# Two-layer transformer kernel: the v projection of the last two layer-1 chunks by seven block products instead of eight, and an emission clock that counts free PSUM banks

## The chip, the core and the metric

The kernel runs on one NeuronCore of a Trainium2 chip. The metric is the device time of one launch in microseconds (us), the median of three runs. PE is TensorE (matrix multiplications; PEld is its weight load), DVE is VectorE, ACT is ScalarE, POOL is GpSimd, SP is SyncE, which here only issues DMAs.

## The reference, cut to what matters

`x` is 2048 tokens by 1024. Each of two layers adds an attention part A and a gated part B, both with the same weights in both layers:

```python
def _A_ref(x, wqkv, wo):          # 32 heads of 32; 8 keys, 2 apart, behind each token
    q, k, v = (x @ wqkv) split in three      # wqkv: 1024 x 3072
    ...                                      # softmax over 8 gathered keys, sum of 8 gathered values
    return o @ wo
def _B_ref(x, w1, w3, w2):        # w1, w3: 1024 x 3584; w2: 3584 x 1024
    return (silu(x @ w1) * (x @ w3)) @ w2
x = x + _A_ref(_layernorm(x), ...)
x = x + _B_ref(_layernorm(x), ...)
x = x + _A_ref(_layernorm(x), ...)
x = x + _B_ref(_layernorm(x), ...)
```

What the change touches is `x @ wqkv`, its last third (v), in layer 1.

## The kernel before

**Units.** The tokens are cut into four chunks of 512; a unit `u` is a layer and a chunk, so u = 0 to 3 is layer 0 and u = 4 to 7 is layer 1. After the four q, k, v products of layer 0, the main loop runs part B of each unit (`b_stage`), and after part B of u = 1, 2, 3, 4 it makes q, k, v of unit u + 3, a chunk of layer 1 (`q_part`, once for each of q, k, v). Every `q_part` takes eight output tiles of 128 rows, each from eight matmuls of 512 columns (L836), evacuated from PSUM by one ACT copy (L840), and written to DRAM; the attention reads q, k and v back from DRAM. One chunk's q, k, v is called a qkv stage here, and its three thirds the q, k and v third.

**Seven products.** From unit 2 on, part B doesn't multiply in the plain way. A product of 2 by 2 blocks is made from seven block products instead of eight (a scheme of the Strassen family): P1, P5, P6, P2 with weights from a tile `early`, P7, P3, P4 with weights from a tile `late`. The sums of weight blocks were made once, earlier (`weight_sums`, `differences`: ACT scales blocks into `big`, DVE adds them, POOL's DMAs store them in DRAM as `t_d`). The sums of the activations are four DVE additions over `xnT` (`norm_sums`, L298), the last of which, for P7, overwrites half of `xnT`. `pipeline` (L1034) runs groups of seven products (each eight matmuls of 256 columns, L1052), the first four products of group i interleaved with the last three of group i - 1. Between products stand small steps: ACT copies P1's result to a second bank (L1064, "B copy"), saves P5 (L1069) and P6 (L1073); DVE adds P6 to the bank of P5 (L1076) and makes one of the four outputs, the "corner", from P7 and P5 (L1088 or L1090). P6 and P2 wait for the B copy, P3 for L1076, P4 for the corner.

**Order.** PE, DVE, ACT and SP each execute their instructions in the order of the program. That order is decided while the kernel is built, by a clock `now` with a cost for each piece of work. Steps of attention, of the norms and of the sums stand in queues as generators; `background(until)` emits the DVE steps that end before the next DVE step of the main line is due, and `act_background` does so for ACT. So a wrong cost only shifts where a step stands, and an engine that reaches a step too early waits, with all that is queued behind it. The norm of a later unit on ACT is `act_norm`: two measuring passes per 128 tokens (L318), seven tiny POOL operations, then an applying pass (L345) and a DMA transpose into `xnT`.

**Attention.** DVE makes scores (L590, L510 and smaller) and values (L665 and smaller) of half chunks, in order; ACT makes one Exp per half chunk (L629), which needs another ACT table than the Silu of part B (L1227), so a table load stands before and after it. PE multiplies the outcome by `wo` (`o_tile`, L771).

**Buffers.** Weight tiles rotate over six buffers (`wp`), released by `release` and loaded by SP in the order of the list `seq`. PSUM has six banks for matrix products (tag `mm`) and two at the side (tag `sd`, for `wo` products and attention logits). The clock knows nothing of banks before the change. `hT` is part B's hidden tile, and the staging for q, k, v of layer 1.

Of the kernel before, what the change touches and what calls it, by code (L numbers as in the profile page):

```python
# [17 lines left out]
def kernel(  # L18
# [137 lines left out]
    opened = [0]  # L156

    def side_tile(*args, **kw):

        while opened[0]:  # L160
            assert head(makes) is not None
            take(makes)
        return side.tile(*args, **kw)

    def bank(name):
        if name == "po":
            return side_tile([P, 512], FP32, name=name, tag="sd")
        return psum.tile([P, 512], FP32, name=name, tag="mm")
# [48 lines left out]
    size2 = const.tile([P, 16], FP32, name="size2")  # L217
    total = const.tile([P, 1], FP32, name="total")
# [4 lines left out]
    h16 = hT[:].bitcast(FP16)  # L223
    t2_d = [dram.tile([P, 7, (b - a) // 2, 512], FP16, name=f"t2_d{i}") for i, (a, b) in enumerate(fsplits)]
    t_d = [[dram.tile([P, 14, KT // 2, P], FP16, name=f"t_d{m}_{g}") for g in range(NG)] for m in range(2)]
    qkv_d = [[dram.tile([P, KT, S], BF16, name=f"qkv_d{l}_{i}") for i in range(3)] for l in range(2)]
# [74 lines left out]
    adds, acts, makes, reads, parts, sizes = [], [], [], [], [], []  # L301
# [61 lines left out]
    def act_background():  # L363
        for queue in (acts, sizes, parts, reads):
# [211 lines left out]
    def score_steps():  # L576

        V = nc.vector
        for g, (l, h) in enumerate(halves):
# [20 lines left out]
            def gather_heads(t, parts_=parts_):  # L600
                at["L"] = L = side_tile([P, W, BLK], FP32, name="L", tag="sd")
                for i in range(parts_):
# [24 lines left out]
            def exps():  # L627
                V.tensor_tensor(L[:], L[:], mx[:].unsqueeze(1).to_broadcast([P, W, BLK]), op=ALU.subtract)
                nc.scalar.activation(E[:], L[:], ACTF.Exp, scale=scale)  # L629
                at["E"] = act(0.65, now["dve"] + 0.1, "exp")  # L630

# [47 lines left out]
    for u in range(len(units)):  # L679
# [14 lines left out]
        if 1 <= u and u + 3 < len(units):  # L694
            seq += [("qkv", which, h) for which in range(3) for h in range(2)]
    w_tiles, w_at, due, used = [], {}, [], [0]

    def load_weight(pieces=1):
# [25 lines left out]
        else:  # L724
# [4 lines left out]
            if rest[0]:  # L729
                got = {}  # L730
                parts.append([weight_size(*rest[0], w, at, got), None])
                reads.append([weight_sums(*rest[0], w, got), None])
# [22 lines left out]
    def o_tile():  # L755
# [12 lines left out]
        for hh in range(2):  # L768
            ps = bank("po")
            for t in range(KT):  # L770
# [6 lines left out]
            dve(0.64, r)  # L777
# [6 lines left out]
    def queue_q(q):  # L784
# [4 lines left out]
        
# [30 lines left out]
    def q_part(l, c, which, ws, then=()):  # L820
# [8 lines left out]
        for t0 in range(0, KT, SG):  # L829
            i = (c * 3 + which) * KT // SG + t0 // SG  # L830
            i = i % (7 if l == 0 else 8) * SG
            sgt = big[:, i * CH:(i + SG) * CH].bitcast(BF16).rearrange("p (a t) -> p a t", a=SG) if l == 0 else hT[:, i:i + SG, :]
            for t in range(t0, t0 + SG):
                ps = bank("ps")
                for kk in range(KT):
# [6 lines left out]
                if first:  # L842
                    nc.scalar.copy(kT[:, t, HALO:], ps[:, 0:TCH])
                    done = act(0.3)
                if t < t0 + SG - 1:
                    pe_requests(2)
            nc.sync.dma_start(qkv_d[l][which][:, t0:t0 + SG, c * CH:(c + 1) * CH], sgt)
            landed = dma(256, done)
            if l == 0:
                stored[:] = landed, landed  # L850
# [6 lines left out]
        if which == 1:  # L857
            plain_left.discard(("Q", l, c))
        if which == 2:
# [56 lines left out]
    pending, stored, made, held = [0] * 2, [0.0] * 2, set(), []  # L916
    junk = hsum[:].bitcast(BF16).rearrange("p k t -> p (k t)")

    def differences(m, g, a, r):

        b = blocks[a]
# [3 lines left out]
        pending[a] -= 1  # L925
        nc.gpsimd.dma_start(t_d[m][g][:, 4 * a:4 * (a + 1)], b[:, 0:4])
        nc.gpsimd.dma_start(t_d[m][g][:, 8 + 3 * a:8 + 3 * (a + 1)], b[:, 4:7])
        stored[a] = now["dve"] + 7.0

    def finish_sums(done):  # L930

        while not done():
            if head(reads) is not None:
                take_act(reads)
            elif head(parts) is not None:
                take_act(parts)
            elif head(makes) is not None:
                take(makes)
# [62 lines left out]
    def sums_of_w2(i, f, ws, loaded):  # L1001

        while "at" not in got2 or all(pending):
# [31 lines left out]
    def pipeline(key, groups, consume, done, last, fill=None):  # L1035
# [6 lines left out]
        def acc():  # L1042
            return psum.tile([P, 2, HT], FP32, name="st", tag="mm")
# [12 lines left out]
        def head_part(i, name):  # L1056
            G = groups[i]
            s5, su, s22 = snaps[i % 2], snaps[2], snaps[3]
            if name == "P1":
                G["early"] = weight("early")  # L1060
                G["A"] = acc()
                r = run(G, name, G["A"], True)
                G["B"] = acc()
                nc.scalar.copy(G["B"][:], G["A"][:])  # L1064
                G["tB"] = act(0.5, r)
            elif name == "P5":
                G["D"] = acc()
                r = run(G, name, G["D"], True)
# [9 lines left out]
            elif name == "P2":  # L1078
                r = run(G, name, G["B"], False, G["tB"])
                release(1)  # L1080
                consume(G, 0, G["B"][:], r)
# [11 lines left out]
            elif name == "P3":  # L1093
                r = run(G, name, G["D"], False, G["tD"])
                consume(G, 1, G["D"][:], r)
            else:
                r = run(G, name, G["A"], False, G["tC"])
                release(1)
                consume(G, 2, G["A"][:], r)

        n = len(groups)
        for i in range(n + 1):
# [15 lines left out]
            done(i)  # L1118

    def products(u, f0, f1, hold):  # L1120
# [25 lines left out]
        def output(j, hh, src, r):  # L1146
# [4 lines left out]
            dve(0.69, r)  # L1151
            if l == 1 and lastsplit:
                nc.sync.dma_start(xout[:, n, hh * 512:(hh + 1) * 512], xs)
                dma(128, now["dve"])

        def W(name, j):
# [12 lines left out]
            if name == "P1":  # L1169
                G["A"] = bank("w2")  # L1170
                r = G["1"] = matmuls(G["A"], True)
                G["B"] = bank("w2")
# [240 lines left out]
```

## Time and profile before

| what | value |
|---|---|
| median of three runs (lowest, highest) | 1533.35 us (1532.43, 1533.71) |
| the profiled execution's own time | 1532.7 us |
| its span, first to last instruction | 1531.0 us |
| busy in the span: PE, PEld | 1518.1 us (99%), 989.5 us |
| busy in the span: DVE, ACT, POOL | 1201.8 us (78%), 884.1 us (58%), 153.7 us |
| granted TensorE clock | 1.000 |
| DMA | 439.56 MB, 287 GB/s on average |

Busy time is the union of an engine's instructions; an instruction of PE is listed with its whole latency, so its mean is longer than the distance from one matmul to the next. "Idle before" is the time for which the engine stood still just before such an instruction, and the releaser is what ended that. The median of the runs is 2.4 us above the span.

### The profile page before, as it was taken

What the parts mean: (1) busy time and instruction counts of PE and PEld (TensorE: products, weight loads), DVE (VectorE), ACT (ScalarE), POOL (GpSimd) and SP (SyncE); (2) the same over time, 40 slices, a digit from 0 to 9 for tenths busy, and PEclk for the clock granted to TensorE, in tenths of its full rate; (3) what the DMA queues carried; (4) which work ended last, traced back from release to release, by engine and by line L of the source; (5) the groups of instructions that cost most, each with busy time, mean ns of one, the idle gap of its engine ahead of it and who ended that gap; (6) DMA issues with size and microseconds to landing.
All of it is one profiled execution on the core that took longest, in us unless ns stands there. A gap on an engine that the chain in (4) does not pass through costs nothing.

```text
span 1531.0 us, 25095 instructions
## 1 busy us (share of the span) xinstructions
PE 1518.1 (99%) x9594; PEld 989.5 (65%) x9634; DVE 1201.8 (78%) x2126; ACT 884.1 (58%) x1388; POOL 153.7 (10%) x308
## 2 busy tenths in 40 slices
PE   9999999999999999999999999999999999999999
PEld 7666644444444577575786767766677767686865
DVE  4688998889989898989698958898678986435445
ACT  3885476567665357455565564756557445554643
POOL 1210102121211101001011010100111000000000
PEclk9999999999999999999999999999999999999999
DMA  9777969798997888979779997898969988878885
GB/s 321 202 218 215 253 226 330 272 304 289 306 320 247 280 316 294 347 264 303 263 269 324 346 268 282 280 323 302 323 225 333 338 296 282 306 272 334 318 294 203
DMA packets 261432, 439.56 MB, mean 287 GB/s; under 512 B 73856, under 2 KB 201088, under 8 KB 245056
## 3 DMA queue, kind: packets, MB, share of 16 engines
q1 hardware_dynamic: 248464, 390.90, 76.8%
q0 software_dynamic: 12704, 46.93, 8.6%
q8 instruction: 75, 1.23, 0.3%
q14 instruction: 45, 0.37, 0.1%
q10 hardware_dynamic: 144, 0.13, 0.0%
HBM read 345.90 MB, written 67.90 MB: 270 GB/s over the span
## 4 chain that ended last, share of the span: by engine, by line
PE 97%; ACT 1%; issue 1%; DVE 0%; DMA 0%; SPq 0%; ACTq 0%
PE st L1052 32%; PE ps L836 21%; PE w L1165 16%; PE po L771 7%; PE pg L1279 6%; PE pu L1288 6%; PE acc L1310 6%; PE pq L444 1%; PE L L604 0%; DMA wqkv<-in_A_wqkv_dram 0%; ACT L629 0%; ACT L1227 0%; ACT E L629 0%; ACT sg L1227 0%; DVE x_sb L1150 0%
## 5 line engine op out<-in xcount | busy, mean ns | idle before, releaser
L836 PE MATMUL ps<-xnT,wqkv 128*128 128x512 f16 (+1 forms) x1469 | 320.4, 379 | 0.2
L1052 PEld LDWEIGHTS <-early 128*128 128x128 f16 x2688 | 262.6, 98 | 40.4 <-issue 3.5
L836 PEld LDWEIGHTS <-wqkv 128*128 128x128 bf16 x1472 | 210.6, 144 | 108.1 <-issue 2.2
L1165 PE MATMUL w<-t,hT 128*128 128x512 f16 x1008 | 226.0, 379 | 0.6 <-ACT big L1185 0.5
L1052 PEld LDWEIGHTS <-late 128*128 128x128 f16 x2016 | 197.2, 98 | 30.6 <-issue 2.5
L590 DVE TENSOR_TENSOR tree<-qT,kT 128x2048 bf16<-128x2048 bf16 x128 | 156.3, 1221 | 35.8 <-DMA kT<-qkv_d 18.2
L1052 PE MATMUL st<-xnT,late 128*128 128x256 f16 x1344 | 174.2, 273 | 2.2 <-ACT big L1073 2.2
L510 DVE TENSOR_TENSOR tree<-tree 128x1024 bf16<-128x1024 bf16 x256 | 175.6, 686 | 0.9
L1052 PE MATMUL st<-big,early 128*128 128x256 f16 x1344 | 172.3, 273 | 1.6 <-ACT sg L1227 1.1
L1165 PEld LDWEIGHTS <-hT 128*128 128x128 f16 x1008 | 98.2, 98 | 112.9 <-DVE hT L1136 2.0
L1052 PE MATMUL st<-xnT,early 128*128 128x256 f16 x1344 | 165.7, 273 | 0.0
L665 DVE TENSOR_TENSOR tree<-At,vT 128x2048 bf16<-128x2048 bf16 x128 | 156.2, 1221 | 11.9 <-DMA At<-E 10.7
L1064 ACT COPY st<-st 128x512 f32<-128x512 f32 x84 | 48.3, 575 | 128.1 <-PE st L1052 127.4
L771 PE MATMUL po<-wo,oT 128*128 128x512 bf16 x486 | 110.8, 379 | 1.3
L840 ACT CAST hT<-ps 128x512 bf16<-128x512 f32 x96 | 55.8, 585 | 90.6 <-PE ps L836 88.3
L1288 PE MATMUL pu<-xnT,w3t 128*128 128x512 f16 x448 | 105.8, 379 | 0.0
L1279 PE MATMUL pg<-xnT,w1t 128*128 128x512 f16 x448 | 105.8, 379 | 0.0
L1310 PE MATMUL acc<-w2t,hT 128*128 128x512 bf16 x437 | 97.8, 379 | 0.6
L1076 DVE TENSOR_TENSOR st<-st,big 128x512 f32<-128x512 f32 x84 | 58.4, 695 | 46.9 <-ACT big L1073 46.8
L1227 ACT ACTIVATE sg<-st,down_scale 128x512 bf16<-128x512 f32 x126 | 86.6, 687 | 11.6 <-PE st L1052 11.0
L1052 PE MATMUL st<-big,late 128*128 128x256 f16 x672 | 87.1, 273 | 0.0
L771 PEld LDWEIGHTS <-oT 128*128 128x128 bf16 x512 | 50.1, 98 | 55.7
(167 smaller groups left out, 1916.6 us busy)
## 6 DMA issues: line engine op xcount, KB each, us to landing
early<-t_d SPq DMA_DIRECT2D x84, 1024.0 KB, 6.9
late<-t_d SPq DMA_DIRECT2D x84, 768.0 KB, 6.2
t<-t_d SPq DMA_DIRECT2D x42, 1024.0 KB, 7.3
t<-t_d SPq DMA_DIRECT2D x42, 768.0 KB, 5.3
wqkv<-in_A_wqkv_dram SPq DMA_DIRECT2D x28, 1024.0 KB, 8.1
w1t<-in_B_w_dram SPq DMA_DIRECT2D x14, 1024.0 KB, 7.6
w3t<-in_B_w_dram SPq DMA_DIRECT2D x14, 1024.0 KB, 11.0
t_d<-big POOLq DMA_DIRECT2D x28, 512.0 KB, 6.2
```

Of the source, the lines that this page charges most:

```text
L510: nc.vector.tensor_tensor(b, b, buf[:, 4:8, :], op=ALU.add)
L590: V.tensor_tensor(pr, qT[:], kT[:, :, k0:k0 + TCH], op=ALU.mult)
L665: V.tensor_tensor(tm.rearrange("p w (a e) -> p w a e", a=4), At[:].rearrange("p a w e -> p w a e"), win, op=ALU.mult)
L771: nc.tensor.matmul(ps[:], lhsT=oT[:, t, j * P:(j + 1) * P], rhs=wo[:, t, hh * 512:(hh + 1) * 512], start=(t == 0), stop=(t == KT - 1))
L836: nc.tensor.matmul(ps[:], lhsT=ws[kk // KH][:, kk % KH, t::KT], rhs=xnT[:, kk, :], start=(kk == 0), stop=(kk == KT - 1))
L1052: nc.tensor.matmul(out[:, a, :], lhsT=w[:, a, blk, k, :], rhs=rhs[:, k, :], start=start and a == 0 and k == 0, stop=k == KQ - 1, skip_grou ...
L1076: nc.vector.tensor_tensor(G["D"][:], G["D"][:], su, op=ALU.add)
L1165: nc.tensor.matmul(out[:], lhsT=lhs[:, k, j * P:(j + 1) * P], rhs=w[:, k, :], start=start and k == 0, stop=k == nq - 1, skip_group_check=True)
L1227: nc.scalar.activation(sg[:], src, ACTF.Silu, scale=inv)
L1279: nc.tensor.matmul(pg[:], lhsT=w1t[:, kk, fi * P:(fi + 1) * P], rhs=xnT[:, kk, :], start=(kk == 0), stop=(kk == KT - 1))
L1288: nc.tensor.matmul(pu[:], lhsT=w3t[:, kk, fi * P:(fi + 1) * P], rhs=xnT[:, kk, :], start=(kk == 0), stop=(kk == KT - 1))
L1310: nc.tensor.matmul(acc[:], lhsT=hT[:, f, j * P:(j + 1) * P], rhs=tiles[hh][f // nq][:, f % nq, :], start=(f == 0), stop=(f == f1 - f0 - 1))
```

## The change

Three things, in one edit.

1. **v by seven products.** While v of layer 1's first chunk is made (after unit 1's part B), ACT squares and sums the eight 128-row blocks of v's weights (`size_of_v`), one PE product with ones adds them up, and DVE turns the sum into a scale. While the second chunk is made (after unit 2's part B), which now goes v, q, k instead of q, k, v, ACT scales sixteen weight blocks and DVE makes sixteen sums of them, which POOL's DMAs store in DRAM as `t_dv` (`sums_of_v`, `differences`). The two weight tiles of v are held until that is done. For the third and fourth chunk (after units 3 and 4) v is made by `v_products`: two groups through `pipeline`, with loads of `early` and `late` from `t_dv` in place of the plain weights.
2. **A clock that counts banks.** `turn` and `free` keep, for each of the two PSUM tags, when a bank comes free in the clock; taking a bank moves the clock's PE time to that point. Every place that takes or empties a bank now says so.
3. **Small changes of order.** `finish_sums` emits attention steps while it waits; sums of w2 are put ahead of those weight sums that nothing holds; q_part can end with k (`last`) and use a shorter staging ring (`ring`); `differences` can use a third block, in `hT`.

The core of the diff (the many lines that only add a `slot = turns[...]` or a `free(...)`, or declare tiles, are left out):

```diff
+    def turn(tag, bufs):
+        ring = rings[tag]
+        if len(ring) >= bufs:
+            now["pe"] = max(now["pe"], ring[-bufs])
+        ring.append(0.0)
+        return ring, len(ring) - 1
+
+    def free(at, t):
+        ring, i = at
+        ring[i] = t + 0.1
...
+        turns["sd"] = turn("sd", 2)
         return side.tile(*args, **kw)
...
+    def mm_tile(shape, name):
+        turns["mm"] = turn("mm", 6)
+        return psum.tile(shape, FP32, name=name, tag="mm")
...
+    blocks += [hT[:, 9:16, :].bitcast(FP16).rearrange("p b (k c) -> p b k c", k=KT // 2)]
...
-            seq += [("qkv", which, h) for which in range(3) for h in range(2)]
+            seq += [("qkv", which, h) for which in ((0, 1, 2), (2, 0, 1), (0, 1))[min(u, 3) - 1] for h in range(2)]
+            if u > 2:
+                seq += [("early", 2, 0), ("early", 2, 1), ("late", 2, 0), ("late", 2, 1)]
...
         queue_norm(key, units[q][1], range(R))
-        
+        if q > NCH + 1:
+            adds.append([sum_later(key), None])
...
+    def size_of_v(i, w, at):
+        for k in range(KH):
+            yield 1.10, at, lambda: nc.scalar.activation(junk[:, 0:D], w[:, k], ACTF.Square,
+                                                         accum_out=size_v[:, KH * i + k:KH * i + k + 1])
+        if i == 1:
+            total_scale(size_v, up_v, down_v, got_v)
+
+    def sums_of_v(ws, at):
+        while "at" not in got_v:
+            yield "blocked"
+        stored[2] = at
+        for g in range(2):
+            for a in range(2):
+                while pending[1] and pending[2]:
+                    yield "blocked"
+                slot = min((i for i in (1, 2) if not pending[i]), key=lambda i: stored[i])
+                pending[slot] += 1
+                b = blocks[slot]
+                for i, (kh, fh) in ((0, (0, 0)), (1, (0, 1)), (3, (1, 0)), (5, (1, 1))):
+                    t = 4 * g + 2 * fh + a
+                    yield 0.65, max(at, got_v["at"], stored[slot]), lambda: nc.scalar.activation(
+                        b[:, i], ws[kh][:, :, t::KT], ACTF.Copy, scale=up_v[:])
+                makes.append([differences(2, g, a, now["act"] + 0.1, slot), None])
+        made.add("v")
...
+    def v_products(l, c):
+        key = ("Q", l, c)
+        slots, landed = [0], []
+        def stage(G, pair):
+            ...
+        def consume(G, q, src, r):
+            pair, t0 = q % 2, HT * (q // 2)
+            to = stage(G, pair)
+            if q != 3:
+                nc.scalar.activation(to[:, :, t0:t0 + HT], src, ACTF.Copy, scale=down_v[:])
+                r = act(0.57, r)
+            ...
+            if not G["left", pair]:
+                t = 4 * G["g"] + 2 * pair
+                nc.sync.dma_start(qkv_d[l][2][:, t:t + SG, c * CH:(c + 1) * CH], to)
+            ...
+        groups = []
+        for g in range(2):
+            G = dict(m=2, g=g, inv=down_v[:])
+            G["corner"] = lambda G=G: stage(G, 1)[:, :, HT:CH]
+            groups.append(G)
+        pipeline(key, groups, consume, lambda i: between(False, i == 0), True)
+        xnT_free[key] = now["pe"]
...
+            if u == 1:
+                for which in range(3):
+                    ...
+                    ws = [weight("qkv"), weight("qkv")]
+                    if which == 2:
+                        for i in range(2):
+                            lazy.append([size_of_v(i, ws[i], max(w_at[used[0] - 2 + i], now["pe"] - 5.0)), None])
+                    q_part(*units[q], which, ws)
+                    while head(lazy) is not None:
+                        take_act(lazy)
+                    release(2)
+                continue
+            if u == 2:
+                for which in (2, 0, 1):
+                    ...
+                    if which == 2:
+                        ready = max(w_at[used[0] - 1], now["pe"])
+                        reads.append([sums_of_v(ws, ready), None])
+                    q_part(*units[q], which, ws, (), 1, 4)
+                    if which == 2:
+                        continue
+                    if which == 0:
+                        finish_sums(lambda: "v" in made)
+                        release(2)
+                    release(2)
+                force(makes, lambda: not any(pending))
+                continue
+            for which in range(2):
+                q_part(*units[q], which, [weight("qkv"), weight("qkv")], (), 1)
                 release(2)
+            v_products(*units[q])
```

## The prediction

> **What bounds the kernel.** First the page's busy times and its chain of work that ended last:
>
> ```profile
> PE 1518.1 (99%) x9594; PEld 989.5 (65%) x9634; DVE 1201.8 (78%) x2126; ACT 884.1 (58%) x1388; POOL 153.7 (10%) x308
> ...
> PE 97%; ACT 1%; issue 1%; DVE 0%; DMA 0%; SPq 0%; ACTq 0%
> ```
>
> PE is the bound, so the time moves only with PE's work and with its few waits. The groups by line give both kinds of product:
>
> ```profile
> L836 PE MATMUL ps<-xnT,wqkv 128*128 128x512 f16 (+1 forms) x1469 | 320.4, 379 | 0.2
> L1052 PE MATMUL st<-big,late 128*128 128x256 f16 x672 | 87.1, 273 | 0.0
> ```
>
> The means are latencies. The distance from start to start, from the timeline, is 215.8 ns at 512 columns (192 in 41.44 us in the qkv stage of unit 4) and 109.2 ns at 256 (8 in 0.873 us). Next, the table of windows: qkv stages of units 2, 3 and 4, with part B of units 3 and 4 between:
>
> ```profile
> 700.70:742.60 41.90, 41.90 (x197) 27.52 (x196) 33.46 (x57) 23.76 (x37) 7.39 (x12) 1.00 0.90 272
> 742.60:885.00 142.40, 142.17 (x1046) 102.15 (x1049) 129.33 (x222) 84.96 (x136) 9.76 (x23) 1.00 0.88 307
> 885.00:926.90 41.90, 41.90 (x198) 27.49 (x197) 24.09 (x40) 23.89 (x37) 5.62 (x14) 1.00 0.91 269
> 926.90:1072.50 145.60, 142.73 (x1050) 102.15 (x1053) 127.34 (x219) 87.08 (x138) 10.88 (x26) 1.00 0.84 295
> 1072.50:1113.90 41.40, 41.40 (x193) 27.50 (x192) 22.82 (x38) 22.22 (x35) 4.47 (x11) 1.00 1.04 323
> ```
>
> Columns: stretch, length, busy PE, PEld, DVE, ACT, POOL, clock, DMA share, GB/s. In qkv stages PE never stands; DVE is free for 8 to 19 us of each, ACT for 18. In part B, DVE has 13 to 18 us to spare. Last, all waits of PE in this execution:
>
> ```profile
> PE st L1052 <- ACT big L1073: 2.2, 1, 2.2
> ...
> PE st L1052 <- ACT sg L1227: 1.1, 1, 1.1
> PE w L1165 <- ACT big L1185: 0.5, 1, 0.5
> PE st L1052 <- ACT st L1064: 0.4, 1, 0.4
> ```
>
> These four lie in or after unit 2's part B, at 989, 669, 1066 and 1234 us. Each is a jam on ACT around an Exp with its table loads. The timeline of the largest:
>
> ```profile
> 984.19 1.28 ACT L629 ACT_TABLE_LOAD   x1
> 985.48 0.60 ACT L629 ACTIVATE E<-L 128x512 bf16<-128x512 f32 x1
> 986.10 1.28 ACT L1227 ACT_TABLE_LOAD   x1
> ...
> 989.16 0.58 ACT L1073 COPY big<-st 128x512 f32<-128x512 f32 x1
> ...
> 989.79 0.38 PE L1052 MATMUL st<-xnT,late 128*128 128x256 f16 x2 [2.19 <-ACT big L1073]
> ```
>
> **What the Trainium skill says.** "TensorE: Matmul & The Clock Gate", section "Back-to-back issue gap", gives a warm isolated gap of N/2.4 + 2.5 ns: 216 and 109 ns, which the trace meets; halving the columns costs nothing per column. "ScalarE: Activation LUTs", section "What ACT_TABLE_LOAD costs", gives 1283 ns for a load (here 1.28) plus a drain. "PSUM — Partial Sum Buffer", section "PSUM: the matmul accumulator", gives 8 banks: six here serve products, so evacuation can lag by some products before PE stops.
>
> **The products.** Removed: twice 64 matmuls of 512 columns, 64 x 0.2158 = 13.81 us each time. Added: twice 2 groups x 7 x 8 = 112 of 256, 112 x 0.1092 = 12.23. That is 2 x 1.58 = **-3.2 us**. The scale's one PE product is like those of L892, 70 ns plus 92 ns before the next matmul: **+0.2**.
>
> **The measuring (unit 1).** Eight Squares over 1024 columns like L318: 1.06 us and 0.19 for the accumulator. The program's order puts one after each of the last seven copies, and one after the last. Copy to next start 0.48, Square to next start 1.24: 1.72 us, just inside the 1.73 of eight matmuls, so ACT keeps step. But the eighth stands ahead of part B's first B copy (L1064), which before started 0.88 us after the last copy (556.57, 557.45) and let P6 begin without a wait. Now it starts 1.72 after: P6 waits **+0.85** (0 to 1.3).
>
> **The sums (unit 2).** ACT: 16 scalings of 0.71 (L910), two between copies: 0.48 + 2 x 0.62 = 1.72 us, again in step. DVE: 16 x 0.42 (L923) = 6.7 us, where DVE had 8.4 idle, of which 3.6 waited for a transpose and 6.8 for kT, which is not next in the new order. POOL issues eight DMAs of 384 or 512 KB, 6 to 7 us to landing (the t_d rows). ACT's third set of scalings reuses a block about 6.5 us after its sums: it may wait up to 1 us, with copies behind it, which free banks cover. The two v weight tiles come free at about 730 instead of 715, so SP loads part B's first four tiles at about 732 instead of 719; early takes 6.9 us to land, needed at 742.6: hidden by some 3 us. Exp of half chunk 9 comes some 3 us later, and four copies after it; banks cover it. Cost **0** (0 to 1.5).
>
> **The new v third (units 3, 4).** Per stage, gone: 8 copies x 0.585. ACT gets 6 copies x 0.58 and 6 outputs x 0.69, DVE 4 steps x 0.7 and four sums x 0.69, SP four loads (3.5 MB for 2 MB). Tiles are loaded 10 us or more ahead; part B's first two follow at the start of the third, 12 us ahead. The transposes for part B stand behind them in unit 3: some 8.5 us into the third, needed at 13. In both units DVE reaches P7's in-place sum early and blocks behind k's last product, delaying values by about 4 us; P7 itself comes 4.4 us later. What isn't hidden:
> Unit 3: the order puts an applying pass (L345, 1.24) after the last k copy, ahead of the B copy: P6 waits **+0.85**, by the arithmetic of the Square. In unit 4 both passes stand before the last copy: 0.
> End of each third: P7, P3, P4 of the second group follow each other with nothing between (part B puts w2 products there). P4 starts 0.87 after P7 and needs the corner, 0.16 + 0.75. Counting DVE's order from the start of the third with the rows' spacings, the corner ends at 12.25 in unit 3 (P4 due 12.2) and 11.9 in unit 4 (due 11.35): **+0.1 and +0.65** (0 to 1.5 each).
>
> **The old waits.** DVE is about 12 us later in units 3 and 4, so Exps move. Half chunk 12's goes from the middle of seven-product groups (wait of 2.2) to between two w2 products' copies, with some 1.5 us of slack by the same counting; 13's from the w2 part (0.5) into unit 4's q third, where banks cover it; 15's (0.4) to the w2 part, ahead of copies not needed at once. PE's listed latency hides 0.16 of each: 3.1 + 3 x 0.16 = **-3.6**. The wait of 1.1 keeps its order and stays. A moved Exp can find a new jam; the eight of layer 1 cost 4.2 us, 0.5 each, so I put back one: **+0.5** (0 to 3). The bank clock's own effect is in this: PE's and DVE's order is the same up to unit 1's v, so it moves nothing before.
>
> **Sum:** -3.2 + 0.2 + 0.85 + 0.85 + 0.1 + 0.65 - 3.6 + 0.5 = -3.65. The profiled execution took 1532.7, its span 1531.0; the same difference on the median 1533.35 gives **1529.7 us**.
>
> **Rivals.**
> A, no change: moved Exps jam elsewhere as much as they did. Then -3.65 - 0.5 + 3.6 = -0.55: **1532.8**. For it: ACT has 13 Exp and norm pieces in part B between units 2 and 5. Against: two of three new places have slack.
> B, more gain: the hand-over waits (2.45) don't occur, because ACT runs ahead by as much: **1527.2**. Against: the orders above are fixed.
> C, slower: DVE's lag. Its added work in units 2 to 4 (6.7, and twice 5.6, and twice 4 blocked) is about 26 us against idle time of 13 to 18 per part B. If the lag doesn't drain, L1076 comes late in group after group and P3 waits some 0.7 us for each: at eight groups a unit for two units, 11 us: 1529.7 + 11 = **1541**. It decides once DVE is 100% busy through a part B; at 87 to 91% it isn't.
> That the products aren't saved is excluded: the program has 128 fewer matmuls of L836 and 224 more of L1052.
>
> **How the numbers follow.** A measurement tells 0.2%, 3.07 us, from no change. Main case 0.52 (own range 1528 to 1531.5), A 0.25, B 0.13, C 0.10. Faster: six tenths of the main case, all of B, some of A: 0.48. Same: the rest of the main case and A: 0.42. Slower: C: 0.10. The range of 8 in 10 takes half of B, all of A and what C gives if it sets in late: 1527.5 to 1534.5.
>
> **What would show it.** Right: PE's matmul counts as above, v thirds of 12.3 to 13.2 us, PE waiting on the B copy for about 0.85 us at the starts of unit 2's part B and unit 3's v third, no wait of 2.2 us in unit 4. Wrong: PE waiting for DVE (L1076, oT, x_sb) or for weight loads, DVE over 95% in a part B, or Exp waits over 1.5 us at new places.

## The result, and the profile after

The changed kernel takes **1538.93 us** (median of four runs, 1538.22 to 1539.60); the kernel before, run beside it, 1532.89 (1531.49 to 1533.71). The ratio is 1.0040, with a 95% interval of 1.0023 to 1.0058. So the change costs 6 us where 3.65 of gain were forecast; the range ended at 1534.5.

The profiled execution took 1538.6 us, its span 1536.9. Line numbers have moved: L869 is the plain product (L836 before), L1118 a matmul of the seven-product scheme (L1052), L989 the scaling of v's weights (like L910, now L944), L958 the sums (L923), L631 the logits on PE (L604). The page's busy times and its chain of work that ended last, and the plain products:

```profile
PE 1520.8 (99%) x9732; PEld 993.7 (65%) x9732; DVE 1217.8 (79%) x2163; ACT 913.9 (59%) x1428; POOL 163.8 (11%) x316
...
PE 85%; DVE 7%; ACT 4%; DMA 2%; issue 1%; POOL 0%; SPq 0%; ACTq 0%; DVEq 0%
...
L869 PE MATMUL ps<-xnT,wqkv 128*128 128x512 f16 (+1 forms) x1344 | 294.2, 380 | 0.0
```

The products were saved as counted: 1344 plain matmuls, where the program before has 1472 (its trace recorded 1469 of them). But the chain is no longer PE's alone: DVE, ACT and DMA hold 13% of it, where they held 1%. PE's waits (engine, line waited for: total, times, longest, us):

```profile
PE L L631 <- DVE psm L540: 2.7, 1, 2.7
PE st L1118 <- DVE big L1157: 1.9, 2, 1.1
PE st L1118 <- ACT st L1132: 1.7, 4, 0.6
PE st L1118 <- ACT big L1142: 1.3, 3, 0.6
...
PE st L1118 <- ACT sg L1338: 1.1, 1, 1.1
PE w L1273 <- ACT big L1296: 1.0, 3, 0.5
```

The old waits of 2.2 and 0.4 us are gone, and that of 0.5 went from 1066 to other places; in their stead stand one of 2.7 and fourteen of 0.15 to 1.1. Cut at the starts of the qkv stages on PE (the distance between first matmuls, from both timelines), the difference falls into these stretches:

| stretch | before, us | after, us | difference | predicted |
|---|---|---|---|---|
| up to unit 1's qkv stage (the same orders) | 514.18 | 513.22 | -0.96 | 0 |
| unit 1's qkv stage (the Squares) | 42.14 | 42.14 | 0 | 0 |
| part B of unit 2 | 144.38 | 147.29 | **+2.9** | +1.05 |
| unit 2's qkv stage (scalings and sums) | 41.92 | 46.00 | **+4.1** | 0 |
| part B of unit 3 | 142.35 | 144.45 | **+2.1** | 0 |
| units 3 and 4's qkv stages, parts B of units 4 and 5 | 372.57 | 370.24 | -2.3 | -4.7 |
| the rest | 273.46 | 273.54 | +0.1 | 0 |

(The first stretch varied between 512.7 and 514.4 in the profiles of this study; its -0.96 is no effect.) The loss sits where the preparation is, not where the seven products are. In the table of windows, the stages and parts B of units 2 to 4 (stretch, length, busy PE, PEld, DVE, ACT, POOL, clock, DMA share, GB/s):

```profile
702.65:748.66 46.01, 43.27 (x198) 27.75 (x197) 34.75 (x68) 38.79 (x51) 13.40 (x18) 0.96 0.77 237
748.66:893.11 144.45, 142.61 (x1049) 102.19 (x1048) 130.54 (x222) 85.79 (x139) 11.03 (x26) 1.00 0.93 329
893.11:935.00 41.89, 41.34 (x252) 29.93 (x251) 23.03 (x39) 27.05 (x42) 5.84 (x14) 1.00 0.82 245
935.00:1077.49 142.49, 141.93 (x1043) 101.47 (x1042) 130.67 (x224) 84.21 (x136) 11.16 (x22) 1.00 0.90 318
1077.49:1119.30 41.81, 41.81 (x258) 30.48 (x257) 24.54 (x40) 27.78 (x43) 7.73 (x14) 1.00 0.98 306
```

In unit 2's stage ACT is busy for 38.8 of 46 us, where it had 23.8 of 41.9 before, and the granted clock is 0.96. DVE never passes 92% in these parts B, so it is not the bound. What happens in the stage shows in the timeline, ACT and DVE first, then PE:

```profile
710.36 2.43 ACT L989 ACTIVATE big<-wqkv,up_v 128x512 f16<-128x512 bf16 x2
712.69 0.58 ACT L873 CAST hT<-ps 128x512 bf16<-128x512 f32 x1
713.15 2.38 ACT L989 ACTIVATE big<-wqkv,up_v 128x512 f16<-128x512 bf16 x2
...
715.56 1.68 DVE L958 TENSOR_TENSOR big<-big 128x512 f16<-128x512 f16 x4 [2.62 <-ACT big L989]
...
721.10 1.68 DVE L958 TENSOR_TENSOR hT<-hT 128x512 f16<-128x512 f16 x4 [2.92 <-ACT hT L989]
...
738.36 0.62 PE L631 MATMUL L<-psm,gather 128*32 128x512 bf16 x4 [2.74 <-DVE psm L540]
```

A scaling takes 1.2 us, not 0.7. ACT needs 2.79 us for two scalings and a copy (710.36 to 713.15), where PE makes a product in 1.73; DVE stands for the scalings with the scores of half chunk 9 queued behind; PE in turn stands for the last of those scores, because the four small matmuls that make the logits are in its own queue. Free banks, which the prediction counted on, don't help an engine whose own next instruction waits. Then the clock falls; windows of the same stage:

```profile
735.25:738.36 3.11, 0.37 (x2) 0.09 (x1) 2.99 (x6) 3.11 (x4) 0.63 (x2) 0.90 0.89 227
738.36:741.30 2.94, 2.94 (x10) 1.14 (x10) 0.00 (x0) 2.94 (x5) 0.00 (x0) 0.53 1.08 318
741.30:748.66 7.36, 7.36 (x36) 4.86 (x35) 5.75 (x11) 4.04 (x8) 1.07 (x2) 1.00 1.03 334
```

For 2.9 us after the stall PE runs at half its clock: matmuls of 512 columns start 427 ns apart instead of 215.8. The stall from start to start is 2.9 us, and the slow matmuls and the late logits add the other 1.2 of the stage's 4.1.

### The profile page after: what moved, and what is told of

Same layout as the page of the kernel before. It is cut to its first block, busy times and chain, and to the rows that moved or that the text cites. A ratio compares the mean times of both kernels' runs of the same rounds, so it can differ in the third digit from the quotient of the medians.

```text
span 1536.9 us, 25459 instructions
## 1 busy us (share of the span) xinstructions
PE 1520.8 (99%) x9732; PEld 993.7 (65%) x9732; DVE 1217.8 (79%) x2163; ACT 913.9 (59%) x1428; POOL 163.8 (11%) x316
## 3 DMA queue, kind: packets, MB, share of 16 engines
q8 instruction: 76, 1.25, 0.3%
## 4 chain that ended last, share of the span: by engine, by line
PE 85%; DVE 7%; ACT 4%; DMA 2%; issue 1%; POOL 0%; SPq 0%; ACTq 0%; DVEq 0%
PE st L1118 29%; PE ps L869 17%; PE w L1273 12%; PE po L802 7%; PE pg L1394 6%; PE acc L1429 6%; PE pu L1405 6%; DVE tree L616 1%; DVE hT L1243 1%; PE pq L470 1%; DMA qkv_d<-hT 1%; ACT xn L344 1%; DVE tree L536 1%; DVE hT L1349 1%; DMA xnT<-xn 1%
## 5 line engine op out<-in xcount | busy, mean ns | idle before, releaser
L1118 PEld LDWEIGHTS <-early 128*128 128x128 f16 x2816 | 275.3, 98 | 43.3 <-issue 4.3
L869 PE MATMUL ps<-xnT,wqkv 128*128 128x512 f16 (+1 forms) x1344 | 294.2, 380 | 0.0
L869 PEld LDWEIGHTS <-wqkv 128*128 128x128 bf16 x1344 | 192.4, 144 | 100.0 <-issue 3.9
L1118 PEld LDWEIGHTS <-late 128*128 128x128 f16 x2112 | 206.4, 98 | 34.3 <-issue 4.9
L1118 PE MATMUL st<-xnT,late 128*128 128x256 f16 x1408 | 182.4, 273 | 3.2 <-DVE big L1157 1.9
L1118 PE MATMUL st<-big,early 128*128 128x256 f16 x1408 | 180.7, 273 | 3.1 <-ACT st L1132 1.7
L1118 PE MATMUL st<-xnT,early 128*128 128x256 f16 x1408 | 173.6, 273 | 0.0
L802 PE MATMUL po<-wo,oT 128*128 128x512 bf16 x512 | 115.7, 379 | 0.0
L1118 PE MATMUL st<-big,late 128*128 128x256 f16 x704 | 91.2, 273 | 0.0
L538 DVE TENSOR_TENSOR tree<-tree 128x512 bf16<-128x512 bf16 x192 | 80.2, 418 | 0.0
```

The source lines that it names most:

```text
L538: nc.vector.tensor_tensor(b[:, 0:2, :], b[:, 0:2, :], b[:, 2:4, :], op=ALU.add)
L802: nc.tensor.matmul(ps[:], lhsT=oT[:, t, j * P:(j + 1) * P], rhs=wo[:, t, hh * 512:(hh + 1) * 512], start=(t == 0), stop=(t == KT - 1))
L869: nc.tensor.matmul(ps[:], lhsT=ws[kk // KH][:, kk % KH, t::KT], rhs=xnT[:, kk, :], start=(kk == 0), stop=(kk == KT - 1))
L1118: nc.tensor.matmul(out[:, a, :], lhsT=w[:, a, blk, k, :], rhs=rhs[:, k, :], start=start and a == 0 and k == 0, stop=k == KQ - 1, skip_grou ...
```

## The experiments

Two theories at the start. **S:** the scalings, which read every eighth column, cost 1.22 us instead of 0.71, and this makes the loss. **O:** the orders that the new bank clock writes make it. Where a table gives stretches, they are those of the table above.

**e1, the stride taken away.**

```diff
-                        b[:, i], ws[kh][:, :, t::KT], ACTF.Copy, scale=up_v[:])
+                        b[:, i], ws[kh][:, :, t * P:(t + 1) * P], ACTF.Copy, scale=up_v[:])
```

> The 16 scalings of v's weights read 128 neighbouring columns instead of every eighth one; size, place and order of every instruction are those of the changed kernel (the sums are of the wrong columns, so the output is not the reference's). Theory S (the stride): one scaling takes 0.71 us instead of 1.22, ACT keeps step in unit 2's qkv stage, the wait for the logits of half chunk 9 (2.7 us) and the reduced clock behind it go, the stage takes 42 us instead of 46, and the total falls by 4 to 6 us, to about 1533.5 us. Theory O (the orders that the new clock wrote are to blame): 1 us or less is won, total above 1537.5.

Measured: 1533.81 us (1532.08 to 1538.35; ratio to before 1.0013, 1.0006 to 1.0019), some 5 us less than the changed kernel (4 by the ratios, each to the kernel before run beside it). The groups by line, apart by form, of the changed kernel (L989, and L944, which scales w1 and w3), then of this one:

```profile
L944 ACT ACTIVATE big<-w1t,up_scale 128x512 f16<-128x512 bf16 x56 | 36.3, 711 | 7.1 <-DMA t_d<-big 6.9 <-DVE up_scale L904 0.3
L989 ACT ACTIVATE big<-wqkv,up_v 128x512 f16<-128x512 bf16 x8 | 9.7, 1267 | 0.0
L989 ACT ACTIVATE hT<-wqkv,up_v 128x512 f16<-128x512 bf16 x8 | 9.5, 1251 | 0.0
```

```profile
L989 ACT ACTIVATE big<-wqkv,up_v 128x512 f16<-128x512 bf16 x8 | 5.4, 738 | 0.0
L989 ACT ACTIVATE hT<-wqkv,up_v 128x512 f16<-128x512 bf16 x8 | 5.4, 720 | 0.0
```

The same operation on the same tile sizes: the page's form "128x512 f16<-128x512 bf16" doesn't tell the two apart, only the code does (`t::KT` against `c0:c0 + P`). With neighbouring columns unit 2's stage takes 41.92 us, just what it took before, and part B of unit 3 142.65 instead of 144.45: a wait of 0.56 us for the B copy and one of 1.25 for the corner at 770, in the same orders, are gone with the lateness that caused them. So the stride costs 4.08 + 1.80 = 5.9 us by the two profiles, of which e1's is its fastest run. S is shown for this part: with the same orders on ACT, DVE and PE and neighbouring columns, nothing of it is left. The other stretches stay: part B of unit 2 147.29, units 3 to 5 370.18.

**e5, what a stride costs.** The four sets of four scalings read at a distance of 1, 2, 4 and 8 columns.

```diff
-                        b[:, i], ws[kh][:, :, t::KT], ACTF.Copy, scale=up_v[:])
+                        b[:, i], ws[kh][:, :, 0:P * (1 << (2 * g + a)):1 << (2 * g + a)], ACTF.Copy, scale=up_v[:])
```

> The four sets of four scalings read 128 columns at a distance of 1, 2, 4 and 8 columns (2, 4, 8 and 16 bytes); nothing else is changed, and the sums are of the wrong columns. Theory L (what costs is a new line of 16 bytes for each element): 0.71 us at distances 1, 2 and 4, 1.22 at 8. Theory N (every read that isn't contiguous costs double): 0.71 at 1, 1.22 at 2, 4 and 8. Theory G (the cost grows with the distance): 0.71, 0.8, 0.95, 1.22 or so.

Measured in one run, of 1533.29 us. Its timeline, one line for each distance in this order (start, time of two, us):

```profile
710.92 1.35 ACT L989 ACTIVATE big<-wqkv,up_v 128x512 f16<-128x512 bf16 x2
...
714.34 1.35 ACT L989 ACTIVATE hT<-wqkv,up_v 128x512 f16<-128x512 bf16 x2
...
723.84 1.50 ACT L989 ACTIVATE big<-wqkv,up_v 128x512 f16<-128x512 bf16 x2
...
732.09 2.42 ACT L989 ACTIVATE hT<-wqkv,up_v 128x512 f16<-128x512 bf16 x2
```

2 and 4 bytes apart cost nothing, 8 bytes a tenth, 16 bytes nearly double the time. That is theory L, but for the tenth. The Trainium skill offers a reason: "SBUF — State Buffer", section "Door 1: The DMA port swizzle (why `[64,N]` ≈ `[32,N]`)", speaks of lines of 16 bytes, of which each needs two or more accesses for full bandwidth. At a distance of 8 two-byte elements every line gives one. That the lines are the cause fits the times; no run here shows it apart. (The page also calls 8 bf16 elements a stride that is free; here it is the one that isn't.)

**e2, the scheduler told the true cost.** A fix that suggests itself: the clock thinks that a scaling takes 0.65.

```diff
-                    yield 0.65, max(at, got_v["at"], stored[slot]), lambda: nc.scalar.activation(
+                    yield 1.22, max(at, got_v["at"], stored[slot]), lambda: nc.scalar.activation(
```

> The scheduler's cost of one scaling is 1.22 instead of 0.65; the work is the same, only places change (one scaling between two copies instead of two, half of them after the q third). Theory S, in the form that ACT has too little room: ACT's work in the stage stays the same, but DVE's sums no longer stand ahead of the scores, so the wait of 2.7 us and the slow matmuls behind it go; eight scalings end the q third late and ACT delays the copies that follow, perhaps 2 to 5 us. Total 1534 to 1539 us. Theory O: no different from the changed kernel, 1538 to 1540.

Measured: 1549.61 us (1549.51 to 1550.30), 10 us worse than either theory said. The scheduler now puts one scaling between two copies and makes the rest in one go when q is done. ACT's timeline there, and PE's largest wait:

```profile
734.87 4.74 ACT L989 ACTIVATE big<-wqkv,up_v 128x512 f16<-128x512 bf16 x4
745.56 4.45 ACT L989 ACTIVATE hT<-wqkv,up_v 128x512 f16<-128x512 bf16 x4 [5.95 <-DMA t_dv<-hT]
749.91 2.50 ACT L873 CAST hT<-ps 128x512 bf16<-128x512 f32 x5
...
PE ps L869 <- ACT hT L873: 8.0, 1, 8.0
```

Eight scalings stand in a row, and between the fourth and the fifth ACT waits another 5.95 us until the store of the block that it is to overwrite has landed. So the copies are held back by 15 us, six banks fill, PE stands for 8.2 and runs 2.3 us longer on the low clock: the stage takes 52.58. The deadline (the v tiles must come free before part B's weights are loaded) leaves no room for the true cost: eight scalings are still to be made when q is done.

**e9, only DVE's queue.** The sums, and their stores, are put off by some steps of DVE, with the clock as it was; the orders of ACT and PE are those of the changed kernel to the instruction.

```diff
-        pending[slot] -= 1
-        nc.gpsimd.dma_start(t_d[m][g][:, 4 * a:4 * (a + 1)], b[:, 0:4])
...
+        if m == 2:
+            later.append([(12, 13, 8, 6)[2 * g + a], slot, all_four])
```

> The changed kernel with one thing moved: DVE's sums of v's blocks in unit 2 stand five to ten steps later in DVE's queue (behind the scores of half chunk 9), where their scalings are done; ACT's and PE's orders and every instruction stay. Theory Q (DVE waited in its queue for the slow scalings, and all else followed): the stage of unit 2 takes 42 us although ACT still works 19.5 us on the scalings, no wait for the logits, no slow clock, the waits of 0.56 and 1.25 us at the start of unit 3's part B go too; total that of e1_contiguous, 1533.8. Theory A (ACT's load itself reaches PE, by copies that come late): 44 us or more, total above 1536.

Measured: 1542.16 us (1538.32 to 1543.44): no better. The wait for the logits and the slow clock went, and the stage fell to 43.62, but part B of unit 3 rose from 144.45 to 147.93. Timeline from its start:

```profile
742.63 3.61 PE L874 MATMUL ps<-xnT,wqkv 128*128 128x512 f16 x16 [0.77 <-ACT hT L878]
746.84 1.05 PE L1142 MATMUL st<-xnT,early 128*128 128x256 f16 x8 [0.60 <-DMA early<-t_d]
749.10 1.03 PE L1142 MATMUL st<-big,early 128*128 128x256 f16 x8 [1.21 <-DVE hT L963]
751.06 1.03 PE L1142 MATMUL st<-big,early 128*128 128x256 f16 x8 [0.93 <-DVE rs L669]
...
773.00 1.03 PE L1142 MATMUL st<-xnT,late 128*128 128x256 f16 x8 [2.64 <-DVE big L1181]
```

ACT is still full, and what stands behind the scalings on it comes late: copies, then the two applying passes of the norm (at 734 and 735), so the transposes (DVE waits 8.75 us for them), so the sums of the activations, then the Exp with four copies behind. (The releasers of 749.10 and 751.06 are put down to DVE, but ACT's first copy behind the Exp ends at 749.06 and the B copy at 751.01.) The stage alone lies between the theories, at 43.62; together with part B of unit 3 it is no shorter than in the changed kernel, which is theory A: DVE's queue was only the first place where ACT's load came out. A part of the new loss is the move's own, though: the last four sums now stand on DVE ahead of this half chunk's softmax (747.85 to 749.52), its values start at 764.13 instead of 762.47, and the wait for the corner grew from 1.24 to 2.81. e10 and e11 below are a cleaner pair: with the same small moves, and in e10 the sums put off as well, stage and part B of unit 3 take 187.96 us with the stride (e10) and 184.06 without (e11), so relieving DVE's queue leaves 3.9 of the stride's 5.9.

**e6 and e7, half the instructions.** Each scaling reads two columns of every eight (two columns apart, by the code; not four, as the expectation has it) and writes two blocks at once; e7 also has the bank clock count only from unit 3's part B on.

```diff
-                for i, (kh, fh) in ((0, (0, 0)), (1, (0, 1)), (3, (1, 0)), (5, (1, 1))):
+                for kh, i, step in ((0, 0, 1), (1, 3, 2)):
+                    two = ws[kh][:].rearrange("p k (j h f a) -> p k j h f a", h=2, f=2, a=2)[:, :, :, g, :, a]
...
+                        b[:, i:i + step + 1:step].rearrange("p f k j -> p k j f"), two, ACTF.Copy, scale=up_v[:])
```

> The same blocks are scaled with half the instructions: each reads two columns of every eight, four columns apart in pairs of output blocks[...], and writes two blocks; eight instructions of 1024 elements instead of sixteen of 512. Theory L: 1.2 to 1.5 us each, some 11 us of ACT instead of 19.5, the stage of unit 2 takes 42 us and the total is that of e1_contiguous, about 1533.8. Theory N: 2.3 us each, ACT as full as before, stage 46 us, total 1538 or more.

> e6_pairs, and the bank clock counts only from unit 3's part B on. If the clock's own harm is the three waits of unit 2's part B (0.75, 0.84 and 0.56 us more than before) and its good lies after unit 3 began: 2.1 us below e6_pairs, about 1531.7, and the waits for the corner at 672 us and for the save of P6 at 610 us gone. If the orders after unit 3 shift again with it, anything from 1530 to 1536.

Measured: 1558.6 us (1557.33 to 1559.14) and 1561.96 (1560.76 to 1562.56). Both theories missed. Group of e6:

```profile
L989 ACT ACTIVATE big<-wqkv,up_v 128x1024 f16<-128x1024 bf16 x4 | 19.7, 4931 | 0.0
```

An element costs 4.8 ns, more than three times what it costs in e1 and twice what it costs in the changed kernel. Reading should have become cheaper by e5; new is that neighbouring writes go to two blocks 1 or 2 KB apart. That this is what costs was not tried alone. The stages took 64 and 66 us, so what e7 says of the clock is in part B of unit 2 only: 145.16 against 147.33 in e6.

**e12, half the scalings on POOL,** with the small moves of e10 below.

```diff
+                        if fh:
+                            nc.gpsimd.tensor_scalar(b[:, i], ws[kh][:, :, t::KT], up_v[:], None, op0=ALU.mult)
```

> A version for use, with the reference's result: the changed kernel with the same five small moves, and every second scaling (the right half of the columns) made by POOL instead of ACT, so that ACT has 9.7 us of scalings instead of 19.5. POOL has no such instruction in the traces so far, so its price is open. At up to 1.3 us each POOL keeps step with ACT, the stage of unit 2 takes 42 us, and the total is that of e11_contiguous_waits_removed, about 1531, below the kernel before. At 2.5 us or more each set of sums comes 2.5 us late again, or DVE and POOL get in each other's way, and the total is 1536 or more.

Measured: 1542.08 us (1540.74 to 1542.90). Group by line:

```profile
L996 POOL TENSOR_SCALAR hT<-wqkv,up_v 128x512 f16<-128x512 bf16 x4 | 12.6, 3159 | 0.0
```

2.5 to 3.2 us each (means of the two groups; spans on POOL are rough), and the norm's small steps, which POOL also makes, stand behind them: the applying passes of ACT wait 7.8 and 8.1 us for those, PE 6.4 for the logits, and the stage takes 51.88.

**e4 and e3, the clock.** e4 has the clock and the small changes of order, with v by eight products throughout; e3 is the changed kernel in which taking a bank doesn't move the clock. The edit of e3:

```diff
-            now["pe"] = max(now["pe"], ring[-bufs])
+            pass
```

> The bank clock and the small changes of order alone: v in all four layer-1 chunks by eight products, no measuring, no sums, order q, k, v. Theory S: within 1.5 us of the kernel before (1532.9), since clock and orders do no great harm. Theory O: 2 us or more slower than before, with corner and B copy waits in part B of units 2 and 3.

> The changed kernel, but taking a bank no longer moves the clock. Theory S: unit 2's qkv stage keeps most of its loss (44 to 46 us), since the scalings stay, total within 2 us of the changed kernel's 1538.9. Theory O: the stalls of 0.76, 0.95 and 1.25 us in the parts B of units 2 and 3 go, and with the moved Exp the total falls by 3 us or more, to below 1536.

Measured: e4 1538.12 us (1535.85 to 1539.20; ratio 1.0035, 1.0022 to 1.0047), e3 1538.33 (1537.33 to 1539.66). By stretch:

| stretch | before | after | e4, clock alone | e3, no clock |
|---|---|---|---|---|
| part B of unit 2 | 144.38 | 147.29 | 146.52 | 145.15 |
| unit 2's qkv stage | 41.92 | 46.00 | 41.92 | 46.89 |
| part B of unit 3 | 142.35 | 144.45 | 142.58 | 143.99 |
| units 3 to 5 | 372.57 | 370.24 | 375.75 | 371.05 |

The first row adds up: the clock brings 2.14 (e4 less before), Square and scale 0.77 (e3 less before), together 2.91, and the changed kernel has 2.91. What the clock does there, in the timeline of e4 and, below, of before, at the same point:

```profile
609.02 1.23 ACT L371 ACTIVATE xn<-x_sb,mom 128x1024 f16<-128x1024 bf16 x1
610.15 0.58 ACT L1140 COPY big<-st 128x512 f32<-128x512 f32 x1
...
610.78 1.03 PE L1116 MATMUL st<-xnT,late 128*128 128x256 f16 x8 [0.59 <-ACT big L1140]
```

```profile
609.10 0.58 ACT L1073 COPY big<-st 128x512 f32<-128x512 f32 x1
609.56 1.25 ACT L345 ACTIVATE xn<-x_sb,mom 128x1024 f16<-128x1024 bf16 x1
```

With PE put later by the clock, a pass of 1.24 us seems to fit ahead of the save of P6, and P7 waits 0.76 from start to start. In the same way other steps of DVE go ahead of the corner at 672 (0.95) and of sums for w2 at 691 and 695 (0.5 and 0.3). Theory S had e4 within 1.5 us of before; it is 5 to 6 above. Of that 2.4 are these waits and those in unit 3, and 3.2 fall in units 3 to 5: the old stalls of 2.36 and 0.63 us stayed, the first now with 1.5 us of slow clock behind it, and new ones of 0.8 and 1.25 came. e3 keeps the loss of the stage, as S said. And over the whole kernel taking the clock away wins next to nothing: 2.1 and 0.5 in the parts B of units 2 and 3 are won, 0.9 in the stage and 0.8 in units 3 to 5 lost, and the median falls by 0.6.

**e8, the products alone,** with weights of another matrix, so without measuring, scalings and sums; the clock counts from unit 3 on.

```diff
-            v = t_d[i][n][:, 0:8] if early else t_d[i][n][:, 8:14]
+            v = t_d[i % 2][n][:, 0:8] if early else t_d[i % 2][n][:, 8:14]
```

> v of the last two chunks by seven products with weight blocks of another matrix (so its output is not the reference's): no measuring, no scalings, no sums, order q, k, v in unit 2, the clock counts from unit 3 on. It shows the product scheme without its price. By the prediction's steps: 3.2 us of PE gained, 0.85 and 0.75 of hand-overs lost, old Exp waits gone: 1529 to 1531 us. If the preparation's cost is only the scalings and the last Square, e7_pairs_late_clock is above it by 0.8 to 1.5 us.

Measured: 1536.86 us (1536.75 to 1538.77; ratio 1.0028, 1.0017 to 1.0040), some 6 us above the expectation. Part B and stage of unit 2 and part B of unit 3 are as before (144.39, 41.92, 142.53). But units 3 to 5 take 377.24, 4.7 *more* than before, with the same 3.2 us of matmuls saved. PE's waits:

```profile
PE st L1121 <- ACT sg L1341: 3.0, 2, 1.9
PE st L1121 <- ACT big L1145: 2.1, 3, 1.0
PE st L1121 <- DVE big L1160: 1.1, 2, 0.8
PE w L1276 <- ACT big L1299: 1.1, 2, 0.6
```

Here an Exp falls on the end of the first seven-product part of unit 4's part B (around 988 us), and seven stalls stand between 979 and 1010, 4.2 us in all, of which 3.0 behind the Exp; part B of unit 5 has stalls of 2.06, 0.95 and 1.2. In the kernels with seven products for v, units 3 to 5 took between 369.8 and 377.2 us with the same instructions; what differs is their order and what comes late into them.

**e10 and e11, small waits removed.** The Squares start two at a time; the clock doesn't count in the first half of part B of unit 2; the time up to which attention steps may be emitted ahead of one corner and three w2 sums is cut by 0.6 to 1.2 us. e10 does this to e9, e11 to e1.

```diff
+                for j in (2 * k, 2 * k + 1) if 2 * k < KH else ():
...
-                background(r + 0.8)
+                background(r + 0.8 - (0.7 if key == ("B", 0, 2) and i == 3 and n < 7 else 0.0))
```

> e9_sums_later, and five waits of PE that the trace names are taken away by a small move each: the Squares of unit 1 start two at a time, so that none stands ahead of the B copy (0.63 us); the bank clock doesn't count in the first half of unit 2's part B (0.76 us at 610); one attention step of DVE goes behind the corner at 672 (0.6 of 0.95 us) and behind the w2 sums at 695, 886 and 1070 (0.3, 0.5 and 0.25 us). If each wait is its own: 3.0 us less than e9_sums_later, about 1530.8. If a wait removed turns up again one step later: 1 us less or nothing.

> e1_contiguous (scalings that read neighbouring columns, so the sums are of the wrong columns) with the five small moves of e10_waits_removed, and DVE's sums where the changed kernel has them. If the waits of 0.63, 0.76, 0.95, 0.3, 0.5 and 0.25 us are each their own, as the trace of e1_contiguous lists them: 2.5 to 3.0 us less than its 1533.8, about 1531, which is 1 to 2 us below the kernel before: what the change would have brought with scalings of the price that the prediction took. If a wait removed comes back at the next step, as the wait of 0.59 at 680 and of 1.8 us at 932 in e10_waits_removed suggest: 1533 or more.

Measured: e10 1537.9 us (1536.75 to 1540.21), 4.3 below e9 (by the profiles 1.5 are won in part B of unit 2, where most of the moves are, and 4.2 in part B of unit 3, where the wait of 2.81 for the corner is gone, at which none of them aims; the stage and units 3 to 5 lose 2.0); e11 1532.04 (1530.54 to 1533.11; ratio 0.9995, 0.9987 to 1.0003), 1.8 below e1 (2.7 by the ratios). In e11 part B of unit 2 falls from 147.29 to 145.77: the waits of 0.76 and 0.95 are gone, that of 0.63 is 0.3, but a new one of 0.59 stands at 680, and of 0.47 and 0.3 the first stayed. So of the 3 us that these waits made, 2 to 3 could be had. With scalings of the price that I took, and these waits removed, the change would have been level with the kernel before, and not 3 us faster. A version for use that beats the kernel before was not found.

## Why the prediction was wrong

**The step that failed first is "The sums (unit 2)":** "16 scalings of 0.71 (L910), two between copies: 0.48 + 2 x 0.62 = 1.72 us, again in step", at a cost of 0 (0 to 1.5). The row was the wrong row: L910 reads 128 neighbouring columns, the new line every eighth, and a scaling took 1.26. The term is +5.9 (4.08 in the stage, 1.80 in part B of unit 3), shown by e1, which changes nothing but the columns read. Put into the sum it turns -3.65 into +2.2. The stride stood in the diff; I looked at the size in the row and not at the subscript in the code. (A smaller slip of this step: of the 6.8 us that DVE waited for kT, only 3.5 lie in the stage, since that wait ended at 745.93.)

**In the same step, "banks cover it"** was no argument for the Exp of half chunk 9. What was late was a matmul's operand in PE's own queue. The 2.9 us stall was dearer than its length, as 1 us of slow clock came on top.

**The clock's orders.** "The bank clock's own effect is in this: PE's and DVE's order is the same up to unit 1's v, so it moves nothing before" left out part B of unit 2, which follows: +2.1 there, shown by e3, e4, e7 and e8, and 0.2 to 0.5 in part B of unit 3 (e4 and e3). That is the cost in these two places; over the whole kernel the clock is nearly even (e3). I had compared the orders and seen that they differ from there on, and had priced only the differences around Exps.

**The Square, the hand-over of unit 3 and the tails.** The Square ahead of the B copy cost 0.63 (predicted 0.85), the scale's product 0.14 (0.2), the applying pass in unit 3 0.72 (0.85), the tails 0.13 each (0.1 and 0.65). All lie within their ranges, and are small. The signs of being right that the prediction named came as well: the counts, v thirds of 13.1 and 12.4 us, no wait of 2.2 in unit 4. None of them concerned unit 2's stage, so they could not tell that the main term was missing. Of the signs of being wrong, PE's waits for DVE came, the largest of them for the scores (2.7), which the list didn't have.

**Products and Exps in units 3 to 5.** Predicted -3.2 + 1.6 - 3.6 + 0.5 = -4.7, measured -2.3. The wait of 2.36 at 987 did go. But the Exp in part B of unit 5 made a cluster of 0.36, 0.43, 0.20 and 0.70 between 1173 and 1180, P5 waited 0.51 for late sums at 935, and w2 parts lost 0.28, 0.27 and 0.65: 3.4 us of new jams where 0.5 (0 to 3) had been put back. The likeliest value was much too low, and the bound was passed.

**The terms together.** The forecast of -3.65, plus 5.9 for the stride, 1.9 in part B of unit 2 (the clock's 2.1, with Square and scale 0.3 cheaper than forecast), 0.3 more in part B of unit 3 and 2.4 in units 3 to 5, gives +6.8; the first stretch, which is no effect, and the rest take 0.9 of it, and the profiles differ by 5.9.

**The rivals.** C, the only one on the slower side, had the sign and no more: DVE's lag in units 3 and 4. DVE was at 90 to 92% in parts B and was not the bound there. The side that lost was ACT, at 84% of unit 2's stage; no rival asked what happens if ACT falls out of step, though two steps rested on 1.72 us being just inside 1.73.

## What to carry to other kernels

A row of the profile prices an instruction's form, not its access pattern: before taking a duration over to new code, compare the subscripts, and if they differ, measure the new one alone: here ACT's reads at steps of 16 bytes took 1.21 us instead of 0.675. When an argument ends on "just in step", price the case in which it isn't, down to who stands behind it in each queue. And in a kernel at 99% of its bound, a planner's change of order is worth as much as the work that it was to save: here the same instructions of units 3 to 5 took from 369.8 to 377.2 us in the orders that were tried, and the products saved 3.2.

## What the runs showed of the hardware that I hadn't expected

- **A short stall can slow the clock; how it falls decides.** Of the PE stalls behind the first 20 us in the profiles here, none up to 2.2 us was followed by slow matmuls; of sixteen between 2.36 and 8.2 us thirteen were, for up to 5.9 us and at a price of 0.6 to 2.9 us. The Trainium skill, "TensorE: Matmul & The Clock Gate", section "What's actually happening", names an idle window of about 3.4 us; here a stall of 2.36 us was enough in e4, and not enough in the kernel before, at the same place of the program. The slow distance, 427 ns, is the page's (section "Wait — 56ns, not 53.3ns?"). The traces show what decides. In each of the fourteen, the changes of the granted clock lie whole multiples of 3.413 us apart, so they stand on a fixed grid. Cut into windows of that grid, e4 and then the kernel before look like this (stretch, length, busy PE, PEld, DVE, ACT, POOL, clock, DMA share, GB/s):

```profile
989.20:992.61 3.41, 1.21 (x12) 0.93 (x11) 3.31 (x6) 3.40 (x7) 1.62 (x3) 1.00 1.74 264
992.61:996.02 3.41, 3.41 (x12) 1.44 (x10) 3.37 (x6) 1.66 (x2) 0.65 (x2) 0.50 0.64 202
```

```profile
984.71:988.12 3.41, 2.89 (x27) 2.44 (x25) 1.94 (x3) 3.37 (x5) 0.00 (x0) 1.00 1.02 357
988.12:991.54 3.42, 1.75 (x13) 1.18 (x13) 3.38 (x6) 3.42 (x6) 2.27 (x4) 1.00 1.18 205
991.54:994.95 3.41, 3.41 (x21) 1.93 (x20) 3.38 (x7) 1.75 (x3) 0.00 (x0) 1.00 1.02 410
```

In e4 the stall lies whole in one window; in the kernel before, the border at 988.12 cuts it in two. Behind the first 20 us the fourteen traces hold 6201 such windows at full clock. In 23 of them PE was busy for 1.30 us or less, and the clock was halved in the next window each time; in all others PE was busy for 1.44 us or more, and the clock stayed. The slow clock ended with the first window in which PE was busy for 2.79 us or more; 2.47 was not enough. This is read from the traces; no run was made to try it.

- **ACT's reads** of two-byte elements: 0.675 us for 512 at distances of 2 and 4 bytes, 0.75 at 8, 1.2 at 16. Writing alternately to two blocks 1 or 2 KB apart, with reads in pairs: 4.9 us for 1024; which of the two costs was not tried.
- **POOL** needs 2.5 to 3.2 us for a scaling that takes ACT 1.26 (e12).
- **A table load** of ACT shows as its 1.28 us alone: in the lines of the prediction the Exp starts at 985.48, 0.01 after the load has ended, and the drain that the prediction names beside it isn't seen.
